# One core, mLSTM front and MLP: per-head products as scaled copies on ScalarE, and a new order of the front's events, engines and fillers

## The chip, the cores and the metric

One core of a Trainium2 chip. The metric is the device time of one execution in microseconds; of the kernel before there are three runs. The engines are named as the profile does: PE (TensorE), DVE (VectorE), ACT (ScalarE), POOL (GpSimd), SP (the queue that issues most DMAs).

## What is computed

A recurrent layer and a two-layer MLP behind it, in float32 precision (the MLP's weights come as float64):

```python
# batch 4, heads 8, seq 768, head_dim 40
m_new = np.maximum(f_gate[:, :, t] + m, i_gate[:, :, t])
f_stab = np.exp(f_gate[:, :, t] + m - m_new)
i_stab = np.exp(i_gate[:, :, t] - m_new)
C = f_stab * C + i_stab * np.einsum('bhd,bhe->bhde', vt, kt)
n = f_stab * n + i_stab * kt
h_tilde = np.einsum('bhde,bhe->bhd', C, qt)
denom = np.maximum(np.abs(nq), 1.0)        # nq = n . q
y[:, :, t] = sigmoid(o_gate) * h_tilde / denom
...
x = attn_out.transpose(0, 2, 1, 3).reshape(3072, 320)
h = x @ w_in                                # 320 x 2048
g = np.maximum(h, 0.0) + np.log1p(np.exp(-np.abs(h)))
out = g @ w_out                             # 2048 x 320
```

## The kernel before

**Steps and tiles.** The 768 positions of each batch are cut into six chunks of 128, which makes 24 steps (batch, chunk). Three steps make one tile of 384 tokens, so the MLP has eight tiles. The first six steps (tiles 0 and 1) are "plain" steps, the others "wide" ones; this change touches the plain ones most. The order of the steps is `ORDER`: (1,0), (2,0), (0,0), (3,0), then the rest by batch. Steps are numbered in that order from 0; tiles of the program are named by their batch and chunk or their step.

**One plain step.** Its inputs are `qk` (queries and keys of all heads), `vt` (values with a column of ones, and keys by token) and the decays `fb`. A scan on VectorE makes the decay matrix `pw` (L402) and the weights `gw` of the state update (L407). `gate_values` (L412) makes `vi` = values times the input gates `gT`; `state_values` (L421) makes `vw` = values times `gw`. TensorE makes scores `ga` (L435) and new state parts (L448) from `vw`; `by_decays` (L456) multiplies the scores by `pw`; `keep_states` copies the state parts to `cp`. `decay_old`, `mid_state` and `new_state` (L491 to L515) carry the state of a batch on: old state times the chunk's decay plus `cp`. `values` (L536, L544) makes `gc` from the states and from the scores. `sum_values` (L555) scales one half of `gc` by the factors `fcT` into `y1` and adds the other; `norm` makes the reciprocal `nq`; `scale_gate` (L579) multiplies the output gate by `nq`; `gated` (L584) makes `x`; TensorE transposes it to `xp`; `high_x` and `low_x` split it into a float32r high part (a cast, L719) and a low part (L676), the tile `X`.

**Products with per-head factors.** Five of these multiply each head's 40 or 41 columns by that head's factor per partition: `vi`, `vw`, `y1`, the gate, and the two decays of a state. Before, each is one `tensor_tensor` with the factors broadcast along the columns, on VectorE or POOL.

**Weights.** `single` (L238) turns a tensor of 640 float64 columns into float32 in two ScalarE steps (L248, L253) and two VectorE steps (L255, L257); `weights` and `weights_out` split it into high and low parts (casts at L719; L295, L297, L305). There are eight such pairs of tensors (w_in and w_out), 256 of the 2048 hidden columns each.

**The MLP.** `products` (L854) runs blocks of 128 hidden columns of one tile: eight matmuls into `hp` (L913), two softplus ACTIVATEs on ScalarE (high part `gh` L807, the whole in place L808), a subtraction on VectorE (`gl`, L811), and nine matmuls into three sums `po` (L877), which come two blocks later. Tile 0 runs its blocks 0 to 9 first (the weights are still arriving), then tile 1 all 16, then tile 0 the rest.

**What sets the order.** All instructions of an engine are kept in the order in which the program writes them (`in_order`, L106). The writing is driven by events in a queue: each has a time counted in TensorE's MLP matmuls (negative for the front), looked up in the table `WHEN` (L970); `tick` writes all events due. `PICK` (L1018) says which engine an event's work runs on: V VectorE, G POOL, A ScalarE, S SP. `WARM` (L1017) gives the number of filler matmuls for eleven places (`keep_warm`, L685). A change of these three tables rewrites the order on every engine.

## Time and profile before

| | us |
|---|---|
| median of 3 runs | 452.35 |
| lowest, highest run | 451.31, 455.11 |
| the profiled execution | 451.38 |
| its span in the trace | 449.6 |
| TensorE busy in the span | 436.0 |
| VectorE, ScalarE, POOL busy | 260.1, 199.5, 108.6 |

The page's busy time is what an engine worked in the span; a view by stretches gives the same for any part of it, with the granted TensorE clock (1.00 is the full clock, 2.4 GHz). A timeline lists instructions by start; instructions of one kind that follow each other are merged, and the time in brackets is idle time before the row and who ended it. A view by form gives for each kind of instruction the number, the total busy us and the mean ns of one. A matmul of float32 counts as two records.

### The profile page before, as it was taken

To read this page: it belongs to the slowest core of one execution; us is meant where nothing else is said; L and a number is where in the kernel's file an instruction comes from. 1 tells how busy PE (TensorE), PEld (TensorE's weight loads), DVE (VectorE), ACT (ScalarE), POOL (GpSimd) and SP (SyncE) were. 2 spreads that over 40 slices of the span, in tenths; PEclk is the share of its full clock that TensorE was granted. 3 is DMA by queue.
4 is the path that set the end of the run, shared out by engine and by line. 5 is a ranking of instruction groups with operands and counts; after the bars stand their busy time and mean duration, and the time that the engine had idled before them with its cause. 6 is when DMAs were issued, how large, how long until landed. Compare 5 with 4: busy or idle time off the path is not lost.

```text
span 449.6 us, 12758 instructions
## 1 busy us (share of the span) xinstructions
PE 436.0 (97%) x5348; PEld 417.4 (93%) x5348; DVE 260.1 (58%) x458; ACT 199.5 (44%) x402; POOL 108.6 (24%) x173
## 2 busy tenths in 40 slices
PE   8769999999998999999999999999999999999996
PEld 7658899999998999999999999999999999999996
DVE  6998698758784665465465465365465465332221
ACT  3576466567435333453236333463336332334332
POOL 4541465456421311211211211111211210000000
PEclk9899799999999999999999999999999999999999
DMA  6986764674435554534443533534533430001001
GB/s 201 291 257 210 241 179 139 189 190 124 122 103 159 133 160 116 170 86 122 127 127 93 139 107 89 179 79 128 127 115 102 129 104 20 23 1 44 2 1 44
DMA packets 51801, 55.93 MB, mean 124 GB/s; under 512 B 5312, under 2 KB 41824, under 8 KB 51744
## 3 DMA queue, kind: packets, MB, share of 16 engines
q1 hardware_dynamic: 48720, 51.68, 41.1%
q10 hardware_dynamic: 3024, 3.44, 2.2%
q8 instruction: 42, 0.69, 0.6%
q14 instruction: 15, 0.12, 0.1%
HBM read 46.47 MB, written 8.64 MB: 123 GB/s over the span
## 4 chain that ended last, share of the span: by engine, by line
PE 91%; DVE 3%; DMA 2%; SPq 1%; ACT 1%; issue 1%; POOL 0%; DVEq 0%; ACTq 0%; POOLq 0%
PE hp L913 40%; PE po L877 37%; PE ga L435 3%; PE gc L597 2%; PE po L688 2%; PE ga L448 2%; PE gc L609 2%; DMA yd<-y 1%; DVE pw L402 1%; DMA nw<-yd 1%; PE gc L536 0%; PE fb L386 0%; PE gc L544 0%; DVE sgi L257 0%; PE xp L666 0%
## 5 line engine op out<-in xcount | busy, mean ns | idle before, releaser
L913 PE MATMUL hp<-X,wih 128*128 128x384 f32 x768 | 181.3, 341 | 1.4 <-ACT X L719 1.4
L807 ACT ACTIVATE gh<-hp 128x384 fp32r<-128x384 f32 x128 | 62.8, 491 | 181.4 <-PE hp L913 170.7
L913 PEld LDWEIGHTS hp<-X,wih 128*128 128x128 f32 x768 | 133.0, 188 | 3.5 <-ACT X L719 1.6
L811 DVE TENSOR_TENSOR gl<-hp,gh 128x384 fp32r<-128x384 f32 x128 | 70.9, 555 | 106.3 <-ACT hp L808 106.3
L877 PE MATMUL po<-woh,gl 128*128 128x320 f32 x384 | 81.4, 312 | 1.6 <-DVE gl L811 1.6
L877 PE MATMUL po<-wol,gh 128*128 128x320 f32 x384 | 82.6, 313 | 0.0
L877 PE MATMUL po<-woh,gh 128*128 128x320 f32 x384 | 81.1, 312 | 0.0
L913 PE MATMUL hp<-X,wil 128*128 128x384 f32 x256 | 66.6, 339 | 0.0
L877 PEld LDWEIGHTS po<-woh,gh 128*128 128x128 f32 x384 | 65.5, 189 | 0.4 <-issue 0.2
L877 PEld LDWEIGHTS po<-woh,gl 128*128 128x128 f32 x384 | 62.7, 189 | 2.2 <-DVE gl L811 1.8
L877 PEld LDWEIGHTS po<-wol,gh 128*128 128x128 f32 x384 | 63.2, 189 | 0.6 <-issue 0.2
L808 ACT ACTIVATE hp<-hp 128x384 f32<-128x384 f32 x128 | 62.3, 487 | 0.0
L913 PEld LDWEIGHTS hp<-X,wil 128*128 128x128 f32 x256 | 46.3, 188 | 0.3 <-issue 0.2
L424 POOL TENSOR_TENSOR vw<-vt,gw 128x328 f32<-128x328 f32 x22 | 16.6, 753 | 111.3 <-DVE gw L407 101.3
L402 DVE TENSOR_TENSOR_SCAN pw<-fb,ident 128x512 f32<-128x512 f32 x24 | 29.5, 1227 | 0.3 <-PE fb L386 0.3
L456 DVE TENSOR_TENSOR pw<-ga,pw 128x512 f32<-128x512 f32 x23 | 15.9, 689 | 20.5 <-PE ga L448 18.1
L506 POOL TENSOR_TENSOR c<-c,cp 104x164 f32<-104x164 f32 x20 | 10.4, 518 | 71.2 <-ACT cp L719 71.1
L416 POOL TENSOR_TENSOR values_in<-vt,gT 128x328 f32<-128x328 f32 x17 | 12.9, 758 | 40.9 <-PE gc L609 19.7
L616 DVE TENSOR_TENSOR y<-gc,y 112x512 f32<-112x512 f32 x18 | 12.4, 691 | 17.2 <-PE gc L609 16.7
L435 PEld LDWEIGHTS ga<-qk 40*64 40x64 f32 x736 | 13.8, 141 | 5.0 <-issue 4.7
L642 DVE RECIPROCAL nm<-nm 128x128 f32<-128x128 f32 x18 | 17.2, 953 | 0.6
L719 ACT COPY cp<-ga 104x328 f32<-104x328 f32 (+1 forms) x21 | 8.7, 414 | 18.7 <-DVE pw L456 13.3
(150 smaller groups left out, 438.6 us busy)
## 6 DMA issues: line engine op xcount, KB each, us to landing
vt<-in_vk SPq DMA_DIRECT2D x24, 324.0 KB
qk<-in_qk SPq DMA_DIRECT2D x48, 160.0 KB
fb<-fz_d SPq DMA_DIRECT2D x42, 128.0 KB
wo<-in_w_out SPq DMA_DIRECT2D x8, 640.0 KB
wr<-in_w_in SPq DMA_DIRECT2D x8, 512.0 KB
eg<-in_oT SPq DMA_DIRECT2D x6, 576.0 KB
yd<-y SPq DMA_DIRECT2D x36, 96.0 KB
out<-ob ACTq DMA_DIRECT2D x21, 160.0 KB
```

The costliest lines, as they stand in the source:

```text
L402: nc.vector.tensor_tensor_scan(z.pw.rearrange(flat), z.fb.rearrange(flat), ident4.rearrange(flat), 0.0, ALU.mult, ALU.add)
L416: pick(f"vi{z.id}", "G").tensor_tensor(vi, z.v1, gT[:, z.c, :, z.b].unsqueeze(3).broadcast_to([128, NQ, HG, E]), op=ALU.mult)
L424: pick(f"vw{z.id}", "G").tensor_tensor(z.vw, z.v1, z.gw.unsqueeze(3).broadcast_to([128, NQ, HG, E]), op=ALU.mult)
L435: nc.tensor.matmul(z.ga[y * Q : (y + 1) * Q, x, (i * NQ + q) * Q : (i * NQ + q + 1) * Q], z.k[rows, g, ts], z.q[rows, g, ts], start=True, ...
L456: nc.vector.tensor_tensor(pw, z.ga[:, :, 0:CP0], pw, op=ALU.mult)
L616: nc.vector.tensor_tensor(y2, z.gc[0 : PP + EP, :, 0:CP0], y2, op=ALU.mult)
L642: nc.vector.reciprocal(nm, nm)
L807: nc.scalar.activation(gh, hp, AF.Softplus)
L808: nc.scalar.activation(hp, hp, AF.Softplus)
L811: nc.vector.tensor_tensor(gl, hp, gh, op=ALU.subtract)
L877: nc.tensor.matmul(po[j], a[:, j * 128 : (j + 1) * 128], w[:, f, :], start=(first and left[j] == 2), stop=(last and left[j] == 0),)
L913: nc.tensor.matmul(hp, a, r, start=(i == 0), stop=(i == len(seq) - 1))
```

## The change

**What it does.** A new helper `scaled` makes a product with per-head factors. On VectorE or POOL it is the old `tensor_tensor`; on ScalarE it is one ACTIVATE for each head (Copy, with the factor of that head as a scale read from memory): eight for `vi`, `vw`, `y1` and the gate, four for a state. All five kinds of products call it, so the decays of a state, which were fixed to POOL, and `y1`, which was fixed to VectorE, get an engine from the table too. In `products` an assertion that a block's weights are written becomes a loop that writes events until they are, and a block takes its PSUM buffer `hp` at its first matmul. The tables `WHEN`, `WARM` and `PICK` are set anew. In the new table 18 products of eight heads and 6 of four stand on ScalarE, all in plain steps or in the states that they leave. Fillers go from 45 to 38.

```diff
+    def scaled(name, default, to, of, by):
+        e = pick(name, default)
+        a, b, w = to.shape[1:]
+        if e is not nc.scalar:
+            e.tensor_tensor(to, of, by.unsqueeze(3).broadcast_to([to.shape[0], a, b, w]), op=ALU.mult)
+            return
+        for i in range(a):
+            for j in range(b):
+                e.activation(to[:, i, j], of[:, i, j], AF.Copy, scale=by[:, i, j : j + 1])
...
-        pick(f"vi{z.id}", "G").tensor_tensor(
-            vi, z.v1, gT[:, z.c, :, z.b].unsqueeze(3).broadcast_to([128, NQ, HG, E]), op=ALU.mult
-        )
+        scaled(f"vi{z.id}", "G", vi, z.v1, gT[:, z.c, :, z.b])
...
-        pick(f"vw{z.id}", "G").tensor_tensor(z.vw, z.v1, z.gw.unsqueeze(3).broadcast_to([128, NQ, HG, E]), op=ALU.mult)
+        scaled(f"vw{z.id}", "G", z.vw, z.v1, z.gw)
...
-            nc.gpsimd.tensor_tensor(heads(z.cm), heads(z.old), fl(z, 0), op=ALU.mult)
+            scaled(f"old{z.id}", "G", heads(z.cm), heads(z.old), fl(z, 0))
...
-            nc.gpsimd.tensor_tensor(heads(c), heads(z.cm) if z.c > 0 else z.cp[:, :, 0], fl(z, 1), op=ALU.mult)
+            scaled(f"new{z.id}", "G", heads(c), heads(z.cm) if z.c > 0 else z.cp[:, :, 0], fl(z, 1))
...
-        nc.vector.tensor_tensor(
-            y1[lo], gc[lo, :, 0:c0].rearrange("p x (g e) -> p x g e", e=E),
-            fc.broadcast_to([L - z.q0 * Q, 2, 4, E]), op=ALU.mult,
+        scaled(
+            f"y1{z.id}", "V", y1[lo], gc[lo, :, 0:c0].rearrange("p x (g e) -> p x g e", e=E),
+            fcT[lo, z.c, z.b].rearrange("p (x g) -> p x g", x=2),
         )
...
-        pick(f"sg{z.s}", "G").tensor_tensor(z.sig, z.sig, z.nq.broadcast_to([128, H, D]), op=ALU.mult)
+        sig = z.sig.unsqueeze(1)
+        scaled(f"sg{z.s}", "G", sig, sig, z.nq.rearrange("p h o -> p o h"))
...
+    def wait_for(names):
+        for x in names:
+            while x not in did:
+                tick(queue[0][0])
...
-                assert all(f"w{f // 2}_1_{k}" in did for k in range(5 + (w is wol)))
+                wait_for(f"w{f // 2}_1_{k}" for k in range(5 + (w is wol)))
...
-            hp = ps_h.tile([128, T], F32, tag="hp", name=f"hp{t}_{f}")
...
-                assert all(f"w{f // 2}_0_{k}" in did for k in range(5 + (i > 3 or (t, f) == (1, 0))))
+                wait_for(f"w{f // 2}_0_{k}" for k in range(5 + (i > 3 or (t, f) == (1, 0))))
+                if i == 0:
+                    hp = ps_h.tile([128, T], F32, tag="hp", name=f"hp{t}_{f}")
...
-    WARM = {0: 9, 1: 0, 2: 5, 3: 2, 4: 3, 5: 8, 6: 0, 7: 3, 8: 12, 9: 3, 10: 0}
-    PICK = {'vi0': 'V', 'vw0': 'V', 'vw2': 'V', 'sg1': 'V', 'cp2': 'V', 'sg2': 'V', 'wi00': 'G', 'mgo0': 'V', 'vi3': 'V',
...
+    WARM = {0: 10, 1: 0, 2: 2, 3: 0, 4: 2, 5: 7, 6: 8, 7: 0, 8: 6, 9: 0, 10: 3}
+    PICK = {'vi0': 'A', 'wi00': 'G', 'wm00': 'V', 'wm01': 'V', 'wl1': 'V', 'ol0': 'V', 'wl2': 'V', 'wl3': 'V', 'new4': 'V',
...
```

**What moves: ScalarE at the end of the front.** On ScalarE, the last instructions ahead of the first softplus. `X0` is the MLP input of tile 0 (its parts come from `xp1`, `xp2`, `xp0` of the first three steps), `woh` and `wih` are high parts of weights, `mag` and `sg` conversion steps, `gh0_0` the first softplus. Before:

```order
L719 CAST wih_100<-sgi1_442 128x2x256
L719 CAST wih_100<-sgi1_442 64x128 x2
L719 CAST X0_489<-xp2_0_514 128x3x128
L253 ACTIVATE sgi2_548<-wr2_356 128x640
L719 CAST X0_489<-xp0_0_553 128x3x128
L763 ACT_TABLE_LOAD
L807 ACTIVATE gh0_0_587<-hp0_0_125 128x384
L808 ACTIVATE hp0_0_125<-hp0_0_125 128x384
```

In the changed kernel (L727 is the old L719, L420 the scaled copies, L815 and L816 the old L807 and L808):

```order
L706 ACTIVATE og_123<-og_123 128x960
L727 CAST X0_551<-xp2_0_537 128x3x128
L727 CAST X0_551<-xp1_0_530 128x3x128
L771 ACT_TABLE_LOAD
L420 ACTIVATE values_in_105<-vt3_0_545,gT_93 128x41 x8
L727 CAST woh_102<-sgo0_528 128x640
L727 CAST X0_551<-xp0_0_601 128x3x128
L248 ACTIVATE magi2_625<-wr2_547 128x640
L727 COPY cp3_0_643<-ga3_0_564 104x328
L727 CAST wih_100<-sgi1_519 128x2x256
L727 CAST wih_100<-sgi1_519 64x128 x2
L253 ACTIVATE sgi2_671<-wr2_547 128x640
```

The table load for softplus and eight scaled copies of step 3's values (`values_in`) now stand ahead of the last cast of `X0`; the high parts of w_in's second tensor (`wih` from `sgi1`) and a conversion step have moved behind it.

**ScalarE among the first blocks.** On ScalarE, from the softplus of block 3 of tile 0 to that of block 4 or 5; step 4 is batch 0, chunk 1. Before:

```order
L807 ACTIVATE gh0_3_860<-hp0_3_814 128x384
L808 ACTIVATE hp0_3_814<-hp0_3_814 128x384
L719 CAST woh_102<-sgo1_625 128x640
L719 COPY cp0_1_891<-ga0_1_816 104x328
L807 ACTIVATE gh0_4_899<-hp0_4_875 128x384
L808 ACTIVATE hp0_4_875<-hp0_4_875 128x384
L719 CAST woh_102<-sgo2_787 128x640
L248 ACTIVATE magi4_928<-wr4_924 128x640
L253 ACTIVATE sgi4_931<-wr4_924 128x640
```

In the changed kernel:

```order
L815 ACTIVATE gh0_3_854<-hp0_3_843 128x384
L816 ACTIVATE hp0_3_843<-hp0_3_843 128x384
L420 ACTIVATE vw0_1_877<-vt0_1_741,gw0_1_808 128x41 x8
L420 ACTIVATE sig3_0_669<-sig3_0_669,nq3_0_839 128x40 x8
L420 ACTIVATE values_in_105<-vt0_1_741,gT_93 128x41 x8
L248 ACTIVATE mago2_911<-wo2_827 128x640
L253 ACTIVATE sgo2_913<-wo2_827 128x640
L815 ACTIVATE gh0_4_957<-hp0_4_902 128x384
L816 ACTIVATE hp0_4_902<-hp0_4_902 128x384
L248 ACTIVATE magi4_969<-wr4_832 128x640
L420 ACTIVATE c1_108<-c0_107,flast_91 104x41 x4
```

Between the softplus of block 3 and that of block 4 stand now 24 scaled copies (`vw`, the gate of step 3, `vi`) and two conversion steps, where two copies stood; four more copies (a state's decay, `c1`) come behind block 4.

**TensorE at the first block.** On TensorE, from the last transpose of the front; `hp0_0` is block 0 of tile 0, `ga3` the scores and state parts of step 3, `pg` the spread of the gates, `po3` with `ident` a filler. Before:

```order
L666 MATMUL xp0_0_553<-ident_80,x0_0_550 64x128 x2
L913 MATMUL hp0_0_125<-X0_489,wih_100 128x384 x4
L913 MATMUL hp0_0_125<-X0_489,wil_101 128x384 x2
L913 MATMUL hp0_0_125<-X0_489,wih_100 128x384 x2
L913 MATMUL hp0_1_592<-X0_489,wih_100 128x384 x4
L913 MATMUL hp0_1_592<-X0_489,wil_101 128x384
L435 MATMUL ga3_0_608<-qk3_0_494 64x64 x16
L913 MATMUL hp0_1_592<-X0_489,wil_101 128x384
```

In the changed kernel (L927 is the old L913, L456 the old L448, L696 the old L688):

```order
L456 MATMUL ga3_0_564<-vw3_0_618,vt3_0_545 40x41
L927 MATMUL hp0_0_651<-X0_551,wih_100 128x384 x4
L927 MATMUL hp0_0_651<-X0_551,wil_101 128x384 x2
L927 MATMUL hp0_0_651<-X0_551,wih_100 128x384 x2
L927 MATMUL hp0_1_679<-X0_551,wih_100 128x384 x4
L132 MATMUL pg_684<-ident_80,ig_134 64x16 x4
L137 MATMUL pg_684<-ident_80,d1_595 128x32
L132 MATMUL pg_684<-ident_80,ig_134 64x16 x4
L137 MATMUL pg_684<-ident_80,d1_595 128x32
L132 MATMUL pg_684<-ident_80,ig_134 64x16 x12
L927 MATMUL hp0_1_679<-X0_551,wil_101 128x384 x2
L696 MATMUL po3_78<-ident_80 128x128 x9
```

The scores and state parts of step 3, which stood inside blocks 1 and 2, now stand ahead of block 0; the gates' spread has moved from behind the first half of block 2 into block 1; 9 fillers follow it there, where 15 stood ahead of it and 3 behind. On SP the first tensor of w_in is now issued ahead of step 0's inputs.

## Rows read from the trace of the kernel before

**Rows 1.** The page: its first line, and TensorE's busy share.

```profile
span 449.6 us, 12758 instructions
...
PE 436.0 (97%) x5348; PEld 417.4 (93%) x5348; DVE 260.1 (58%) x458; ACT 199.5 (44%) x402; POOL 108.6 (24%) x173
```

**Rows 2.** Busy time of each engine by stretch; after the engines: clock, DMA share, GB/s.

```profile
core 0: us, PE busy (x) PEld busy (x) DVE busy (x) ACT busy (x) POOL busy (x), PEclk, DMA share, GB/s
0.00:10.00 10.00, 8.30 (x99) 7.77 (x100) 6.02 (x19) 3.21 (x6) 3.96 (x18) 1.00 0.66 192
...
20.00:30.00 10.00, 6.90 (x139) 5.50 (x132) 9.52 (x22) 5.97 (x10) 5.53 (x8) 1.00 0.84 233
...
150.00:350.00 200.00, 200.00 (x2573) 193.08 (x2572) 110.20 (x189) 82.69 (x168) 38.85 (x68) 1.00 0.45 122
```

**Rows 3.** Timeline of TensorE around the marks: start, us, engine, line, operation, tiles, count.

```profile
31.82 1.21 PE L913 MATMUL hp<-X,wih 128*128 128x384 f32 x4 [1.37 <-ACT X L719]
...
37.27 3.51 PE L688 MATMUL po<-ident 128*128 128x128 f32 x30
...
63.06 0.69 PE L435 MATMUL ga<-qk 40*64 40x64 f32 x32
...
64.12 0.44 PE L913 MATMUL hp<-X,wih 128*128 128x384 f32 x1
...
76.93 0.51 PE L913 MATMUL hp<-X,wih 128*128 128x384 f32 x2
```

**Rows 4.** The same timeline, at the one long wait behind the second mark.

```profile
145.00 0.71 PE L877 MATMUL po<-woh,gl 128*128 128x320 f32 x3 [1.56 <-DVE gl L811]
```

**Rows 5.** By half microseconds, columns as in rows 2: the lower clock's two ends.

```profile
43.50:44.00 0.50, 0.50 (x6) 0.40 (x4) 0.40 (x2) 0.00 (x0) 0.00 (x0) 0.82 0.84 291
...
50.50:51.00 0.50, 0.50 (x17) 0.43 (x10) 0.50 (x2) 0.00 (x0) 0.50 (x1) 0.85 0.87 234
```

**Rows 6.** Groups on POOL and VectorE by form: count, busy us, mean ns, idle.

```profile
L424 POOL TENSOR_TENSOR vw<-vt,gw 128x328 f32<-128x328 f32 x22 | 16.6, 753 | 111.3 <-DVE gw L407 101.3 <-PE hp L913 6.6 <-DMA vt<-in_vk 3.3
...
L580 DVE TENSOR_TENSOR og<-og,nq 128x320 f32<-128x320 f32 x2 | 1.0, 488 | 0.0
...
L402 DVE TENSOR_TENSOR_SCAN pw<-fb,ident 128x512 f32<-128x512 f32 x24 | 29.5, 1227 | 0.3 <-PE fb L386 0.3
...
L305 DVE TENSOR_TENSOR wol<-sgo,woh 128x640 fp32r<-128x640 f32 x5 | 4.7, 936 | 0.3 <-ACT woh L719 0.2
```

**Rows 7.** Timeline of ScalarE in the front: two small pairs, the last cast of X.

```profile
4.35 0.31 ACT L157 ACTIVATE fg<-fg 32x128 f32<-32x128 f32 x1 [1.08 <-DVE fg L154]
4.56 0.29 ACT L158 ACTIVATE ig<-ig 32x128 f32<-32x128 f32 x1
...
14.27 0.18 ACT L175 COPY fcT<-po 128x32 f32<-128x32 f32 x1
14.35 0.44 ACT L719 COPY cp<-ga 104x328 f32<-104x328 f32 x1
...
31.31 0.46 ACT L719 CAST X<-xp 128x384 fp32r<-128x384 f32 x1
```

**Rows 8.** Groups on ScalarE by form, columns as in rows 6.

```profile
L807 ACT ACTIVATE gh<-hp 128x384 fp32r<-128x384 f32 x128 | 62.8, 491 | 181.4 <-PE hp L913 170.7 <-issue 9.1 <-PE po L877 1.4
...
L248 ACT ACTIVATE magi<-wr 128x640 f32<-128x640 f32 x8 | 6.3, 793 | 6.6 <-DMA wr<-in_w_in 6.6
...
L719 ACT CAST wih<-sgi 128x512 fp32r<-128x512 f32 x6 | 3.7, 614 | 0.0
...
L719 ACT CAST woh<-sgo 128x640 fp32r<-128x640 f32 x6 | 4.3, 722 | 1.1 <-DVE sgo L257 1.1
...
L763 ACT ACT_TABLE_LOAD x2 | 2.6, 1283 | 0.0
...
L698 ACT ACTIVATE og<-og 128x960 f32<-128x960 f32 x2 | 2.0, 1003 | 1.2 <-DMA og<-in_o 1.1
...
L719 ACT COPY cp<-ga 104x328 f32<-104x328 f32 x18 | 7.8, 433 | 16.4 <-DVE pw L456 11.0 <-PE ga L448 5.4
```

## Prediction of the time

> **What bounds the kernel now.** I read the page's busy shares first, then the table by stretches, and last the timelines of TensorE and ScalarE around the two marks below. TensorE is busy for 436.0 us of the span of 449.6 [rows 1]. From 150 to 350 us it is busy all 200.00, with ScalarE at 82.69 [rows 2]: there, work moved between the other engines changes nothing. From 20 to 30 us it isn't: TensorE does 6.90 of 10, VectorE 9.52, ScalarE 5.97 [rows 2]. So the front is VectorE's. The marks: the first w_in product of tile 0 starts at 31.82, the first of tile 1 at 76.93 [rows 3]. What is computed behind the second mark is the same in both kernels, so the change is worth the shift of that mark, and what becomes of one wait of 1.56 us at 145 us for a `gl` of VectorE [rows 4].
>
> Between the marks lie 45.1 us. Two things there are not work for the result. One is fillers: 15 matmuls in 3.51 us at 37.27 [rows 3], 0.23 each, and 3 more. The other is the lower clock: the half-microsecond rows show a granted clock of 0.82 at 43.5 and 0.85 at 50.5 [rows 5], with thirteen rows of 0.50 between, that is 1.2 GHz for some 7.0 us, which loses 3.5.
>
> **What the change takes away and adds.** Each product with per-head factors was one instruction, 0.75 us on POOL or 0.49 on VectorE [rows 6]. Now 18 of them are 8 scaled copies on ScalarE and 6 (decays of states) are 4 copies: 168 ACTIVATEs, 128 of them ahead of the second mark.
> Ahead of its last low part of X for tile 0 VectorE loses two such products (0.49 each), a copy of `cp` that I count the same, a conversion step and two low parts of weights (0.94 each as [rows 6] has one): 4.3 us. It gains an `x` (0.5), two small subtractions (0.4 each) and the scan of step 3 with its `gw` (1.23 [rows 6] and 0.2): 2.7. That frees 1.6. But TensorE now has the state products of step 3 ahead of the first w_in product, and they wait for that scan and then for a product on POOL (0.75). So by VectorE alone the first mark stands near 31.5, hardly earlier.
> From the first mark on there are 9 fillers less (2.1); the score and state products of step 3 are done (for a later step they take from 63.06 to 64.12 [rows 3], 1.1); and if the clock stays up, 3.5 come back. 45.1 - 6.7 = 38.4, and 31.5 + 38.4 = 69.9. That is the floor which TensorE and VectorE set for the second mark, 7.0 us earlier than now.
>
> **ScalarE decides.** The trace has no copy with a factor from memory, so its price from start to start (call it p) is bounded. Below: the 32-column copy of `fcT` starts at 14.27 and the next instruction at 14.35 [rows 7], 0.08. Above: an ACTIVATE of 128 columns takes 0.31 us whole [rows 7], if nothing overlapped. Between them: that ACTIVATE starts at 4.35 and the next at 4.56 [rows 7], 0.21. I take 0.21, as the only pair of small ACTIVATEs in the trace; it has 87 columns more than a piece, and a piece has an operand more. The pair shows too that an instruction starts 0.10 before the last one ends, so every duration below counts less 0.10.
> By the columns alone a piece would be cheaper: from 640 to 384 columns ([rows 8], 0.72 and 0.49) a column is worth 0.9 ns, so 87 columns fewer make 0.13.
> Against that stands a rule of the Trainium skill, "ScalarE: Activation LUTs", What ACT_TABLE_LOAD costs: a pointer operand adds about 93 ns to an ACTIVATE, and neighbours overlap by about 93. Its price without a pointer agrees with the 0.72 us of a 640-column cast [rows 8]; the pointer's price no row here shows. By it a piece is an estimated 0.22 us from the next, and the sum below would be 1.3 us higher.
>
> Leg 1 runs from the first piece to the last cast of X for tile 0. The pieces wait for step 0's values, which SP now queues behind the first tensor of w_in: 1.5 MB in all, and the 192 GB/s of the first 10 us [rows 2] put that at 8 to 10. I take 10.0. ScalarE then has 48 pieces, and by [rows 8], less 0.10: three `cp` 1.0, a copy of factors 0.1, two Exps like the cast of 640 columns 1.3, a 64-row cast 0.2, two table loads (whole) 2.6, two sigmoids 1.8, four conversion steps 2.8, three casts of X (0.46 whole [rows 7]) 1.1, one of `woh` 0.6. That is 11.5. The cast ends at 10.0 + 11.5 + 48 p = 31.6 with p = 0.21; in the kernel before it starts at 31.31 [rows 7]. I found no input that comes later than ScalarE there.
> Leg 2 runs from there to the last cast of X for tile 1: 14 conversion steps 9.7, casts of w_in for three and a half tensors 4.0, two of `woh` 1.3, two `cp` 0.7, ten softplus pairs 7.8, gate copies 0.3, two casts of X 0.8, which is 24.6, and 80 pieces. It waits for others by an estimate from the same durations 3.6 us: 1.3 for the gate products (the first two w_in blocks stand ahead of them on TensorE), 0.9 for step 3 and block 2, 0.3 for a reciprocal, 1.1 for the last `x` and its transposes. To the first product of tile 1 another 0.2. So 28.4 + 80 p.
> Sum: 10.0 + 11.5 + 28.4 + 128 p = 49.9 + 128 p, with p = 0.21 76.8 against 76.93, 0.1 us earlier. Behind the mark 40 pieces, 8.4 us, lie under stretches where ScalarE has more than half its time free; the 1.56 us wait may go or stay, and I let it stay. The profiled execution took 451.38 us; 0.1 less is 451.3. The median of the three runs is 0.97 above the profiled one, so I forecast 452.
> Bounds of the sum: any p up to 0.156 gives the floor, 451.38 - 7.0 = 444.4. p = 0.31 gives 89.6, 12.7 later, 464.
>
> Edits at nothing. POOL and VectorE lose work in stretches where TensorE or ScalarE sets the pace; without that cover their relief is the 1.6 us above. On SP the stored gates wait for the second sigmoid, and behind them stand the second w_out tensor, the later decays and their loads. All these are first read after 38 us, so 2 or 3 us of delay are covered; a us beyond that is a us on the second mark. Blocks now take their PSUM buffer after their weights' events, which moves an allocation and no instruction. The lower clock may stay or go: nothing while ScalarE sets the pace, up to 3.5 us otherwise.
>
> **Rivals.** First, cheap pieces. At p of 0.156 or less ScalarE keeps ahead, the second mark is at 69.9 and the time 444.4, about 445 for a median. For it: the 0.08 of the small copies, the 0.13 by columns, and ScalarE's idle 4 of 10 us now. Against: none of those has a factor from memory.
> Second, slower: a piece overlaps less, or pays more for its factor. The place is the same queue, above all where the sets for `vw`, the gate and `vi` of step 4 stand in a row ahead of the softplus of block 4, while block 4's w_out products wait. From p = 0.246 the loss is over 1% (0.035 x 128 = 4.5 us); at 0.255 it is 5.6, 457, or 458 for a median. For it: the whole duration of 0.31. Against: the pairs in [rows 7] overlap.
> Third, the pieces are cheap but the new order gives its gain back: the clock falls again after the gate products (3.5) and the front is 3 us longer, since 48 pieces stand ahead of the X casts. That ends within 1% too, at 451; its mark is TensorE at 1.2 GHz after 35 us while ScalarE is idle.
>
> **How the numbers follow.** About 1% is what a measurement here can tell from no change. The forecast, with ScalarE as the pace and level with the old order, and the third rival, which ends in the same place, have 0.46 together (0.38 and 0.08). The forecast's own range is 448 to 456, p from 0.18 to 0.24. Cheap pieces have 0.36, the slower case 0.18. Faster, same and slower are these three. The 8 in 10 reach from 443, the floor less the wait at 145, to 458, the second rival at 0.255.
>
> **What would show it.** Right: pieces 0.2 us apart; the first w_in product of tile 0 between 31 and 34 us; from there to the second mark ScalarE over 90% busy, TensorE under 85%, with waits for ScalarE at the value products of steps 4 and 5; the first product of tile 1 between 75 and 79. Wrong: pieces under 0.16 apart and tile 1 before 72; pieces 0.25 or more apart; a first product of tile 0 before 29, which would say that I misread VectorE's chain; new waits of TensorE behind 150 us.

## Result and profile after

| | kernel before | changed kernel |
|---|---|---|
| median of 20 runs, us | 453.19 | 456.23 |
| lowest to highest, us | 450.87 to 457.17 | 454.27 to 458.41 |
| ratio, 95% interval | | 1.006 (1.0037 to 1.0084) |
| profiled execution, its span, us | 451.38, 449.6 | 457.89, 455.8 |

The changed kernel is 0.6% slower, 3.0 us in the medians. The time stays within 1%, as forecast, but the forecast was 0.1 us less, and it went the other way; 456.23 lies just above the forecast's own range of 448 to 456. Below, the first mark is the first w_in product of tile 0, the second mark that of tile 1. The page, and the table by stretches with the columns of [rows 2]:

```profile
span 455.8 us, 12870 instructions
...
PE 440.7 (97%) x5334; PEld 421.7 (93%) x5334; DVE 261.8 (57%) x466; ACT 230.0 (50%) x562; POOL 92.2 (20%) x149
```

```profile
20.00:30.00 10.00, 9.36 (x145) 7.54 (x142) 7.62 (x21) 9.53 (x27) 0.82 (x1) 0.50 0.91 240
50.00:60.00 10.00, 9.81 (x115) 8.63 (x114) 6.29 (x15) 9.93 (x38) 2.19 (x3) 1.00 0.84 236
60.00:70.00 10.00, 7.20 (x149) 6.46 (x148) 7.43 (x15) 10.00 (x32) 3.23 (x3) 0.83 0.57 169
150.00:350.00 200.00, 200.00 (x2574) 193.08 (x2573) 108.71 (x187) 80.11 (x166) 38.09 (x68) 1.00 0.44 122
```

From 150 to 350 us nothing has changed: TensorE is busy all the time [rows 2]. From 50 to 70 us ScalarE is now busy 19.93 of 20 and TensorE 17.01. The timeline of TensorE at the two marks, beside [rows 3]:

```profile
35.95 0.96 PE L927 MATMUL hp<-X,wih 128*128 128x384 f32 x4
40.83 3.79 PE L696 MATMUL po<-ident 128*128 128x128 f32 x18
83.82 0.84 PE L927 MATMUL hp<-X,wih 128*128 128x384 f32 x2
```

The first mark stands 4.1 us later, the second 6.9 us. Two stretches say more than the marks, up to the first one and between the two. Before:

```profile
8.00:31.82 23.82, 17.01 (x414) 14.26 (x410) 21.80 (x44) 14.51 (x25) 14.06 (x17) 0.93 0.92 271
31.82:76.93 45.11, 45.07 (x619) 40.45 (x619) 37.84 (x66) 26.47 (x53) 18.97 (x24) 0.92 0.66 199
```

Changed:

```profile
8.00:35.95 27.95, 23.19 (x489) 19.50 (x485) 22.43 (x44) 24.44 (x70) 9.80 (x11) 0.76 0.88 246
35.95:83.82 47.87, 43.06 (x539) 38.97 (x537) 34.21 (x67) 42.33 (x137) 13.29 (x15) 0.91 0.68 188
```

Between the marks TensorE had no gap; now it has 4.8 us of them, and ScalarE works 42.3 of 47.9 in place of 26.5 of 45.1. ScalarE's timeline from the softplus of block 3 to the next cast of X (a row with x8 is eight pieces, and each row starts where the last one can):

```profile
52.83 1.87 ACT L420 ACTIVATE vw<-vt,gw 128x41 f32<-128x41 f32 x8
54.60 1.85 ACT L420 ACTIVATE sig<-sig,nq 128x40 f32<-128x40 f32 x8
56.35 1.85 ACT L420 ACTIVATE values_in<-vt,gT 128x41 f32<-128x41 f32 x8
58.11 0.77 ACT L248 ACTIVATE mago<-wo 128x640 f32<-128x640 f32 x1
...
60.90 0.97 ACT L420 ACTIVATE c<-c,flast 104x41 f32<-104x41 f32 x4
61.78 0.76 ACT L253 ACTIVATE sgi<-wr 128x640 uint32<-128x640 uint32 x1
62.44 0.46 ACT L727 CAST X<-xp 128x384 fp32r<-128x384 f32 x1
```

A piece starts (58.11 - 52.83) / 24 = 0.22 us after the last. The list of TensorE's waits names what that does:

```profile
PE gc L544 <- DVE X L684: 2.8, 1, 2.8
PE xp L672 <- POOL x L592: 2.3, 2, 1.8
```

The 2.8 us are at 60.7: the values of step 4 need the PSUM buffer in which step 3's `xp` still stands (both use the one buffer of the tag `pa`). VectorE's low part frees it at 63.5 and had waited for the cast at 62.44, which stood in ScalarE's queue behind the rows above: `xp` was written by 58.5. The second wait, 1.8 us at 79.6, ends when POOL has made `x` of step 5 from a gate whose eight pieces run on ScalarE from 78.55 to 80.41.

**The same kernels profiled again.** The two profiled executions are 6.5 us apart, the medians 3.0. So both were taken once more, unchanged. For the changed kernel:

> The changed kernel once more, unchanged, on the chip of the three runs beside it. Its profiled execution lay 1.7 us above its median and that of the kernel before 1.8 below its own. If the marks are those of any execution: first product of tile 0 at 35.5 to 36.5, first of tile 1 at 83 to 84.5, ratio 1.004 to 1.009. If half of the shift of the mark was that one execution: mark at 80 to 82.5 with a time of 455 to 456.

Measured: ratio 1.0095 (1.0063 to 1.0126); the profiled execution took 455.78 us with its second mark at 82.00, as the second possibility had it. For the kernel before:

> The kernel before once more, unchanged, for a second profile of its front. If its front comes out differently from one execution to the next: first product of tile 0 at 33 to 34.5 (33.96 in the run with fewer fillers, whose order is the same up to there) in place of 31.82, mark of tile 1 at 78 to 79.5, time 452.5 to 454. If the one profile is typical: 31.5 to 32.3 and 76.5 to 77.5.

Both profiles, up to the first mark and on to the second; the kernel before:

```profile
8.00:34.38 26.38, 20.83 (x413) 17.63 (x409) 21.68 (x44) 14.66 (x25) 14.04 (x17) 0.74 0.83 248
34.38:78.03 43.65, 43.63 (x618) 39.30 (x619) 37.75 (x66) 26.46 (x53) 19.00 (x24) 0.96 0.71 204
```

the changed kernel:

```profile
8.00:35.89 27.89, 23.44 (x476) 20.03 (x474) 21.47 (x44) 24.60 (x70) 9.85 (x11) 0.69 0.85 245
35.89:82.00 46.11, 41.36 (x541) 37.28 (x537) 33.71 (x66) 42.19 (x137) 13.87 (x15) 0.94 0.70 195
```

The old front differs from one execution to the next: 31.82 at a mean clock of 0.93, 34.38 at 0.74. The profile that the prediction rests on had a fast one. In this second pair the spans are 450.8 and 453.6, and the 2.8 us are: 1.5 at the first mark, 2.5 between the marks, 1.2 less behind the second (the wait of [rows 4] is gone in both profiles of the changed kernel). That it is close to the 3.0 us of the medians is in part luck: the six executions of the changed kernel beside that profile have a median of 457.89, 5.0 above that of the kernel before, and the profiled one is among the fastest of them. So the change costs 3 to 5 us.

### The profile page after: what moved, and what is told of

It is laid out like the page before. It is cut to its first block, busy times and chain, and to the rows that moved or that the text cites. A ratio compares the mean times of both kernels' runs of the same rounds, so it can differ in the third digit from the quotient of the medians.

```text
span 455.8 us, 12870 instructions
## 1 busy us (share of the span) xinstructions
PE 440.7 (97%) x5334; PEld 421.7 (93%) x5334; DVE 261.8 (57%) x466; ACT 230.0 (50%) x562; POOL 92.2 (20%) x149
## 4 chain that ended last, share of the span: by engine, by line
PE 80%; ACT 10%; DMA 3%; issue 3%; DVE 2%; SPq 2%; POOL 0%; DVEq 0%; POOLq 0%; ACTq 0%
PE hp L927 35%; PE po L890 33%; PE ga L443 2%; PE gc L605 2%; DMA y<-fc_d 2%; PE gc L617 2%; PE ga L456 2%; PE po L696 1%; DMA vt<-in_vk 1%; ACT vw L420 1%; ACT values_in L420 1%; ACT gh L815 1%; ACT vi L420 1%; ACT sig L420 1%; ACT hp L816 1%
## 5 line engine op out<-in xcount | busy, mean ns | idle before, releaser
L927 PE MATMUL hp<-X,wih 128*128 128x384 f32 x768 | 181.8, 341 | 0.0
L815 ACT ACTIVATE gh<-hp 128x384 fp32r<-128x384 f32 x128 | 62.8, 491 | 175.6 <-PE hp L927 165.0
L927 PEld LDWEIGHTS hp<-X,wih 128*128 128x128 f32 x768 | 133.5, 189 | 1.6 <-issue 0.2
L927 PE MATMUL hp<-X,wil 128*128 128x384 f32 x256 | 66.2, 340 | 0.0
L816 ACT ACTIVATE hp<-hp 128x384 f32<-128x384 f32 x128 | 62.3, 487 | 0.0
L927 PEld LDWEIGHTS hp<-X,wil 128*128 128x128 f32 x256 | 46.7, 190 | 0.1
L416 POOL TENSOR_TENSOR vw<-vt,gw 128x328 f32<-128x328 f32 x18 | 13.8, 765 | 112.5 <-DVE gw L407 108.5
L443 PE MATMUL ga<-qk 40*64 40x64 f32 x736 | 17.0, 230 | 1.8 <-PE po L456 0.9
```

The costliest lines, as they stand in the source:

```text
L416: e.tensor_tensor(to, of, by.unsqueeze(3).broadcast_to([to.shape[0], a, b, w]), op=ALU.mult)
L443: nc.tensor.matmul(z.ga[y * Q : (y + 1) * Q, x, (i * NQ + q) * Q : (i * NQ + q + 1) * Q], z.k[rows, g, ts], z.q[rows, g, ts], start=True, ...
L815: nc.scalar.activation(gh, hp, AF.Softplus)
L816: nc.scalar.activation(hp, hp, AF.Softplus)
L927: nc.tensor.matmul(hp, a, r, start=(i == 0), stop=(i == len(seq) - 1))
```

## Experiments

A piece is one scaled copy, a set the four or eight pieces of one product. Two theories. A: ScalarE's queue sets the pace, each piece costs 0.22 us there. B: the new order, its fillers and the lower clock are slow by themselves. All marks in one table (us; the clock is the mean granted clock from 8 us to the first mark):

| run | first mark | clock | second mark | between | ratio (95%) |
|---|---|---|---|---|---|
| before, twice | 31.82, 34.38 | 0.93, 0.74 | 76.93, 78.03 | 45.1, 43.7 | 1 |
| changed, twice | 35.95, 35.89 | 0.76, 0.69 | 83.82, 82.00 | 47.9, 46.1 | 1.006, 1.0095 |
| none on ScalarE | 37.80 | 0.71 | 80.88 | 43.1 | 1.0005 (0.9987 to 1.0023) |
| constant factor | 34.26 | 0.87 | 73.06 | 38.8 | 0.9868 (0.9836 to 0.99) |
| front sets back | 37.55 | 0.71 | 85.08 | 47.5 | 1.010 (1.0067 to 1.0133) |
| later sets back | 37.02 | 0.65 | 79.92 | 42.9 | 0.9982 (0.996 to 1.0005) |
| old order, sets on ScalarE | 41.36 | 0.64 | 92.65 | 51.3 | 1.0566 (1.0492 to 1.064) |
| changed, 17 fillers less | 37.31 | 0.70 | 84.48 | 47.2 | 1.0102 (1.0051 to 1.0154) |
| changed, inputs first | 38.80 | 0.67 | 84.69 | 45.9 | 1.0118 (1.0065 to 1.0172) |
| inputs first, conversion behind | 38.06 | 0.66 | 83.88 | 45.8 | 1.0091 (1.006 to 1.0123) |
| changed, 17 fillers more | 36.72 | 0.88 | 84.05 | 47.3 | 1.0079 (1.0042 to 1.0116) |
| `fcT` first | 36.61 | 0.76 | 82.66 | 46.1 | 1.0103 (1.0032 to 1.0174) |
| 17 fillers more, later sets back | 36.97 | 0.88 | 79.69 | 42.7 | 0.9988 (0.9952 to 1.0024) |
| later sets back, 17 fillers less, inputs first | 37.31 | 0.68 | 84.17 | 46.9 | 1.0067 (1.0034 to 1.010) |
| later sets back, 17 fillers more, `fcT` first | 37.36 | 0.88 | 80.10 | 42.7 | 1.0014 (0.9982 to 1.0045) |
| later sets back, inputs first, conversion behind | 36.15 | 0.70 | 78.90 | 42.8 | 0.9991 (0.9961 to 1.0021) |
| before, 9 fillers less | 33.96 | 0.87 | 77.58 | 43.6 | 0.9987 (0.9948 to 1.0026) |
| old front, new order behind | 34.82 | 0.68 | 80.66 | 45.8 | 1.0016 (0.9972 to 1.006) |

### Which sets cost, and where

The edits take sets out of the table's "A" entries; the engine is then the one of before.

```diff
-    PICK = {'vi0': 'A', ... 'vw0': 'A', 'vi1': 'A', ... 'vi4': 'A', ...
+    PICK = {'vi0': 'V', ... 'vw0': 'V', ...
```

> The changed kernel with all 24 sets of products with factors back on the engines that the kernel before gives them (VectorE or POOL); order, fillers and all other picks as changed. Theory A, ScalarE's queue sets the pace up to the first product of tile 1 (83.82 us in the changed kernel): ScalarE loses 128 pieces of 0.22 = 28 us ahead of that mark, TensorE and VectorE decide there, the mark comes at 70 to 76 and the ratio to the kernel before is 0.975 to 0.99. Rival B, the new order, its fillers and the stretches at the lower clock are what is slow, the pieces are not: the mark stays at 80 or later and the ratio is 1.003 or more.

> The changed kernel with only the six sets of the front (48 pieces: vw of step 0, vi of steps 0 to 3, the gate of step 0) back on the engines of before. Theory A: the last cast of X for tile 0 is no longer behind 48 x 0.22 = 10.6 us of pieces; VectorE's chain sets it, near 30, the first product of tile 0 comes at 31 to 33.5 in place of 35.95, and as ScalarE still carries 80 pieces behind it the mark of tile 1 moves by the same 2 to 4 us, to 79.5 to 82; ratio to before 0.997 to 1.003. Rival B: both marks within 1 us of the changed kernel's, ratio 1.004 or more.

> The changed kernel with only the 18 later sets (80 pieces between the first product of tile 0 and the mark of tile 1, 40 behind it) back on the engines of before, the front's six sets stay on ScalarE. Theory A: the first product of tile 0 stays at 35 to 37, ScalarE loses 80 x 0.22 = 17.6 us behind it, TensorE sets the pace, and the mark of tile 1 comes 39 to 41 us after the first product of tile 0, at 74.5 to 77.5; ratio 0.983 to 0.993. Rival B: the mark stays at 80 or later, ratio 1.003 or more.

The stretch between the marks with the later 80 pieces off ScalarE, and then with only the front's 48 off:

```profile
37.02:79.92 42.90, 39.99 (x539) 36.25 (x537) 38.43 (x71) 25.38 (x53) 18.79 (x22) 0.96 0.73 210
```

```profile
37.55:85.08 47.53, 42.78 (x540) 38.82 (x537) 34.27 (x67) 42.23 (x137) 13.48 (x15) 0.91 0.69 190
```

The later sets cost 3.2 to 5.0 us between the marks (46.1 or 47.9 against 42.9, and 47.5 against 43.1 where the front's sets are off too). There Theory A has the place and the direction right. It has the size wrong: 80 pieces of 0.22 are 17.6 us of ScalarE's queue, and the stretch got 3.2 to 5.0 shorter, to 42.9 and not to 39 to 41. With the sets on VectorE and POOL TensorE waits for those. Its longest waits in the stretch, with the later sets back, and with 17 fillers more besides:

```profile
PE xp L672 <- POOL x L592: 1.4, 2, 1.2
...
PE xp L672 <- POOL x L592: 2.9, 2, 1.7
```

In the front Theory A fails: with its six sets back, the first mark comes 1.6 us later, not 2 to 4 earlier. Some 1.0 us of that is a new wait of step 3's state products for a `vw` on POOL, the same in both runs without these sets (that `vw` needs VectorE's scan, which with none on ScalarE starts at 34.87 in place of 32.75). The rest is not clear of the spread: the same front gave 35.95, 35.89 and 37.02 (the run with the later sets back), and 37.80 and 37.55 without its sets. All off together is level with the kernel before (1.0005). So Theory B falls as an account of the loss: the new order without a piece on ScalarE loses nothing. It gains nothing either, where Theory A expected 1 to 2.5%.

### The price of a piece

```diff
-                e.activation(to[:, i, j], of[:, i, j], AF.Copy, scale=by[:, i, j : j + 1])
+                e.activation(to[:, i, j], of[:, i, j], AF.Copy, scale=1.0)
```

> The changed kernel with the constant 1 in place of the factor read from memory in each scaled copy on ScalarE: the factors of those 24 sets are left out of the computation; number and order of all instructions stay. Theory A with the factor's pointer as the price: pieces start 0.13 apart in place of 0.22, 128 x 0.09 = 11.5 us less in ScalarE's queue, the mark of tile 1 moves from 83.8 to between 72 and 76, ratio to before 0.975 to 0.99. Rival C, any small ACTIVATE costs 0.22 whatever its factor: pieces stay at 0.20 to 0.22, mark and time as in the changed kernel (1.003 to 1.009). Rival B (the order is slow): pieces may be 0.13, the mark stays at 80 or later.

ScalarE, and the stretch between the marks:

```profile
49.84 1.11 ACT L420 ACTIVATE sig<-sig 128x40 f32<-128x40 f32 x8
50.85 1.12 ACT L420 ACTIVATE values_in<-vt 128x41 f32<-128x41 f32 x8
51.87 0.78 ACT L248 ACTIVATE mago<-wo 128x640 f32<-128x640 f32 x1
```

```profile
34.26:73.06 38.80, 38.01 (x539) 34.70 (x537) 34.31 (x66) 34.66 (x135) 13.47 (x15) 1.00 0.85 233
```

A piece is 0.13 now ((51.87 - 49.84) / 16), the factor in memory costs 0.09, and between the marks 38.8 are left. 80 x 0.09 = 7.2; measured are 7.3 against the second profile of the changed kernel and 9.1 against the first. That 7.2 and 7.3 agree is in part luck: the clock stays at 1.00 here, and in the changed kernel's first profile it falls to 0.50 at 64.5 and at 81.5 us, soon after the two waits named above, and at 40.5. Without its factor a piece needn't wait for one either, but such a wait is in the changed kernel's trace between the marks only once, 0.52 us for `nq`. So the price of a piece, with the order untouched, decides some 2% of the time (0.9868 against 1.006 or 1.0095). The Trainium skill, "ScalarE: Activation LUTs", What ACT_TABLE_LOAD costs, has about 93 ns for a pointer operand; the trace agrees with its 0.09.

### The same sets in the old order

```diff
-    WHEN = {...}; WARM = {...}   (changed)
+    WHEN = {...}; WARM = {...}   (before; PICK of before, the same 24 sets on 'A')
```

> The helper with the tables of the kernel before (order, fillers, picks), and only the same 24 sets put on ScalarE. Theory A (the pieces at 0.22 are the price, the new order isn't): ScalarE's queue, 66% to 89% busy around the marks in the kernel before, gets 28 us more ahead of the mark of tile 1; the mark comes at 80 to 88 in place of 76.9 and the ratio is 1.006 to 1.025. Rival D, the loss needs the new order (its later front at 36 to 38 us): in the old order the pieces fit into ScalarE's idle time, mark at 75 to 79, ratio 0.997 to 1.003.

5.7% slower: more than Theory A foresaw, and the rival that the pieces fit into idle time falls. TensorE waits three times for a `vw` on ScalarE, 7.9 us in all. The new order takes most of that cost away.

### The clock and the fillers

```diff
-    WARM = {... 6: 8, 7: 0, 8: 6, 9: 0, 10: 3}
+    WARM = {... 6: 0, 7: 0, 8: 0, 9: 0, 10: 0}
```

> The changed kernel without the 17 filler matmuls on both sides of the first product of tile 0 (8 ahead of it, 9 behind the gate products). Theory D, fillers stand on the chain there: the first product of tile 0 comes 1 to 2 us earlier (34 to 35), the second softplus and with it ScalarE's queue 3 to 5.5 us earlier, mark of tile 1 at 79 to 81, ratio 0.996 to 1.001. Rival A alone (ScalarE's queue is full all the way): mark within 1 us of 83.8, ratio 1.004 to 1.009. Rival E, the fillers hold up the clock: without them 1.2 GHz lasts longer than the 3.2 us around 42, and the mark stays or moves later.

Theory D falls and Rival E's outcome came: first mark 37.31, second 84.48, and a ratio level with the 1.0095 of the changed kernel's second measurement. At 1.2 GHz are now the stretches from 37.0 to 40.5 and from 43.75 to 47.5 us (0.51 and 0.54); from its first mark to 50 us the changed kernel has one, from 40.5 to 44.5, in its first profile and none in its second. The opposite edit puts fillers where TensorE stood idle in the front:

```diff
-    WARM = {... 1: 0, 2: 2, 3: 0, ... 9: 0}; 'k2': -279, 'k3': -234, 'k9': 13.75
+    WARM = {... 1: 4, 2: 8, 3: 4, ... 9: 3}; 'k2': -269.5, 'k3': -253.5, 'k9': -237.5
```

> The changed kernel with 17 more filler matmuls in the front, put where TensorE stood idle ahead of and inside the stretch at 1.2 GHz from 16.8 to 30.8 us (4 ahead of step 0's scores, 8 in place of 2 ahead of step 1's, 4 ahead of step 2's, 3 ahead of step 2's values). Theory F, the clock is what the late front and part of the mark are made of (half clock cost 12.0 us up to the mark in the changed kernel, 5.1 in the kernel before): that stretch shrinks to 7 us or less, first product of tile 0 at 33 to 35, mark of tile 1 at 80.5 to 83, ratio 0.998 to 1.004. Rival A (ScalarE's queue carries the front as well): stretch shorter, yet the last cast of X for tile 0 stays at 33 to 34 and the mark at 83 to 85, ratio 1.004 to 1.009.

> The same 17 more fillers, and the 18 later sets on the engines of before (six sets stay on ScalarE in the front). Theories F and A together: first product of tile 0 at 33 to 35.5, 39 to 42.9 us from there to the mark, which comes at 72 to 78; ratio 0.983 to 0.997. If neither the clock nor the sets matter: mark at 80 or later, ratio 0.998 or more.

The mean clock rises from 0.76 to 0.88, and the marks don't move earlier. The chain of waits of that run (the first of the two) shows why:

```profile
13.01 2.00 PE po L696 x16
...
17.54 1.10 PE po L696 x8
...
22.76 1.65 PE po L696 x6
```

Fillers stand in the chain themselves, 4.8 us of it (15, of which 13 are added ones), and the clock gave back an estimated 0.12 x 28.7 = 3.4, or 5.5 against the 0.69 of the second profile. With the later sets back it is the same: clock 0.65 or 0.88, mark 79.9 or 79.7. So these runs don't separate the clock from the fillers that raise it; they show that the two together gain nothing.

Between the marks the table has more to say. With all later sets on ScalarE and the fillers there unchanged, three runs have a stretch at 1.2 GHz somewhere between 40.5 and 46.5 us and take 47.3 to 47.9 (changed, front sets back, 17 fillers more); four have none and take 45.8 to 46.1 (changed again, `fcT` first, the two with inputs first). So 1.2 to 2.1 us of the loss come and go with the clock, in the same kernel too. With the later sets back that stretch is worth 0.1 to 0.4 (42.9 and 43.1 with it, 42.7 to 42.8 without), since TensorE's waits for POOL grow when it goes.

In the kernel before, as many fillers out as the change takes out:

```diff
-    WARM = {... 7: 3, 8: 12, 9: 3, 10: 0}
+    WARM = {... 7: 3, 8: 6, 9: 0, 10: 0}
```

> The kernel before (old tables, nothing on ScalarE that wasn't there) with 9 of the 18 fillers behind the first mark taken out, as many as the change takes out there. Part of theory A: with the pieces off ScalarE the new order is 2.2 us shorter between the marks than the old one, and the fewer fillers are that gain: mark at 74.5 to 75.5, ratio 0.993 to 0.997. Rival E, the fillers hold up the clock: 1.2 GHz lasts longer than the 7 us of the kernel before, mark at 76.5 to 80, ratio 0.998 to 1.008.

Between the marks 43.6, which is the 43.7 of the kernel before in its second profile. No gain that can be measured, and the prediction had 2.1 us for it.

### What holds up the front

Three moves in the table `WHEN`: step 0's inputs first on SP; the same with two conversion steps of ScalarE behind step 0's pieces; the copy `fcT` ahead of them.

```diff
-    'load0': -286, 'w0_0_0': -292, 'w0_0_1': -282, 'p7': -268
+    'load0': -296.5                                         (first)
+    'load0': -296.5, 'w0_0_0': -275.9, 'w0_0_1': -275.8     (second)
+    'p7': -280.5                                            (third)
```

> The changed kernel with only step 0's inputs issued on SP ahead of the first tensor of w_in, as before. Theory D, the late inputs hold up the front: first piece at 9.5 to 10 in place of 11.05, the first product of tile 0 1 to 1.5 us earlier, at 34.5 to 35, the mark of tile 1 at 82.3 to 83, ratio 1.002 to 1.006. Rival: the first tensor of w_in, now later, and VectorE's conversion behind it take that back, first product and mark within 0.5 us of the changed kernel's.

> The changed kernel with step 0's inputs issued first on SP as before, and now the two ScalarE steps for the first tensor of w_in behind the pieces of vw and vi of step 0, so that these don't wait behind a conversion for a later tensor. Theory H, VectorE's idle time (5.5 us in place of 2.0 between 8 us and the first product of tile 0) is what the front lost, and part of it comes from late inputs: first piece at 9.5 to 10, first product of tile 0 at 34 to 35, mark at 82 to 83, ratio 1.0 to 1.006. Rival: the order on ScalarE and the clock take it back, first product at 35.5 to 37, ratio 1.004 to 1.01.

> The changed kernel with one copy on ScalarE moved, that of the factors fcT (0.18 us), from behind the pieces of vw and vi of step 0 to ahead of them. Theory A for the front (16 pieces stand ahead of what TensorE waits for): TensorE's wait of 1.84 us for fcT ahead of step 1's scores goes, these start 1 to 2 us earlier, the stretch at 1.2 GHz gets shorter, first product of tile 0 at 33.5 to 35.5, ratio 0.998 to 1.005. Rival: step 1's scores then wait for step 0's state copy or weights instead and start within 0.5 us of 15.1; all marks and the time stay, ratio 1.004 to 1.009.

ScalarE at step 0 in the first, then in the second run:

```profile
10.53 0.77 ACT L248 ACTIVATE magi<-wr 128x640 f32<-128x640 f32 x1 [4.23 <-DMA wr<-in_w_in]
11.21 0.76 ACT L253 ACTIVATE sgi<-wr 128x640 uint32<-128x640 uint32 x1
11.87 1.85 ACT L420 ACTIVATE vw<-vt,gw 128x41 f32<-128x41 f32 x8
```

```profile
10.24 1.86 ACT L420 ACTIVATE vw<-vt,gw 128x41 f32<-128x41 f32 x8 [3.15 <-DVE gw L407]
...
15.40 0.18 ACT L175 COPY fcT<-po 128x32 f32<-128x32 f32 x1
```

In the first the pieces come 0.8 us later, since a conversion ahead of them waits for its tensor. In the second they come 0.8 us earlier, but the conversion now stands ahead of `fcT`, and TensorE's wait for that grows from 1.8 to 3.2 us. In the third that wait falls to 0.3 and others take its place (1.6 us for two `cp`, 1.0 for one more). In these three, what was moved ahead on ScalarE was paid for behind. None moved the first mark earlier.

### Versions that might beat both

Three join edits from above: the later sets back, no 17 fillers and the inputs first; the later sets back, 17 fillers more and `fcT` first; the later sets back and the inputs first with the conversion behind.

> The changed kernel with the 18 later sets on the engines of before, without the 17 fillers, and with step 0's inputs issued first. If the parts add up: first product of tile 0 at 33 to 34.5 (37.0 with the later sets moved alone, less 2 for fillers, less 1 for the inputs), from there 39 to 40 us to the mark of tile 1 (42.9 less 2 to 3.5 for the fillers), mark at 72 to 75, ratio 0.985 to 0.993. If the clock falls for longer without the fillers: mark at 76 to 79, ratio 0.994 to 1.0.

> All three together: the factors' copy first, 17 more fillers in the front, the 18 later sets back on VectorE and POOL. If the parts add up: first product of tile 0 at 32 to 34, mark of tile 1 at 71 to 76, ratio 0.98 to 0.993. If the parts share one cause, the clock, it is within 0.003 of the run with the fillers and the sets alone.

> The same order of loads, with the 18 later sets on VectorE and POOL as before. If both gains add up: first product of tile 0 at 34 to 36, 42.5 to 43 us from there to the mark, which comes at 76.5 to 79, ratio 0.988 to 0.997. If the front stays: mark at 79 to 81, ratio 0.995 to 1.001.

Marks of tile 1: 84.17, 80.10 and 78.90. In the first, without the fillers, TensorE runs at 1.2 GHz from the first mark to 49.3 us (mean clock between the marks 0.83), and the stretch takes 46.9 where the later sets back alone took 42.9. The parts don't add up in any of them. The last takes the old front and the new order behind it:

```diff
-    WHEN, PICK, WARM = changed
+    WHEN = before for events up to 21, else changed; PICK = before for steps 0 to 3, else as with the later sets back
+    WARM = {0: 9, 1: 0, 2: 5, 3: 2, 4: 3, 5: 8, 6: 0, 7: 3, 8: 6, 9: 0, 10: 0}
```

> The kernel before up to the first blocks (all events up to 21 matmuls behind the first product, with their engines; 9 fillers fewer behind the first mark), and from there the changed order with the 18 later sets on VectorE and POOL; no set on ScalarE. If the old front (32 to 34 us) and the changed order's 42.7 us between the marks and 2 us less behind them add up: mark at 74.5 to 77, ratio 0.985 to 0.996. If the changed order between the marks needs its own front: mark at 77.5 to 80, ratio 0.996 to 1.004.

1.0016 and 45.8 us between the marks, where TensorE waits 1.3 us for a `wol`, 1.2 for an `x` and 0.6 for a `pw`: behind the old front the changed order does not reach its 42.7 us, as the second possibility had it. No kernel here that does the whole work is faster than the kernel before by more than the measurement can tell; the best is the changed kernel with the later sets back, 0.9982 (0.996 to 1.0005).

## Why the prediction was wrong

**What held.** The place: ScalarE's queue between the marks is what the change costs. By the timeline the sets for `vw`, the gate and `vi` of step 4 in a row are the worst of it, with the wait of 2.8 us behind them; no run moved one of these sets alone. The test set for it was met in part: over the whole stretch ScalarE is 88% busy, not over 90, and TensorE 90%, not under 85; from 50 to 70 us it is 100 and 85. Of the cheap pieces' floor the half between the marks was right: 38.4 was worked out, 38.8 measured at 0.13 a piece. Behind the second mark nothing was lost; 0.7 and 1.2 us were gained.

**The step that failed is the sum of ScalarE's two legs**, 76.8 for the second mark; measured are 83.82 and, in the second profile, 82.00. Its largest fault is the waiting in leg 2, set at 3.6 us. What ScalarE waited for there, in the first profile:

```profile
ACT gh L815 <- PE hp L927: 2.0, 2, 1.8
ACT cp L727 <- PE ga L456: 1.4, 1, 1.4
ACT gT L223 <- PE pg L132: 1.4, 1, 1.4
ACT X L727 <- PE xp L674: 1.3, 1, 1.3
ACT sig L420 <- DVE nq L583: 0.5, 1, 0.5
```

By the sum's terms, in the same profile:
- p was taken as 0.21 from the pair of 128-column ACTIVATEs; it is 0.22. 128 x 0.01 = 1.3. The sentence on the Trainium skill had that number, and the sum by it would have been nearer.
- The first piece started at 11.05, not 10.0 (10.46 in the second profile).
- Leg 1, from there to the last cast of X, is 22.5, against 11.5 + 48 x 0.22 = 22.1: the size is right. That ScalarE alone sets it isn't shown: with none of the sets on it that cast still started at 34.68 (33.55 here), behind a `woh` that had waited 2.5 us for VectorE.
- Leg 2 had 3.6 us of waiting. ScalarE waited 6.6: 1.4 for the state parts of step 3, which stand behind 8 fillers on TensorE; 1.4 for the gates' spread; 2.0 for products, of which 1.8 come behind the 9 fillers that ran at 1.2 GHz (3.79 us); 1.3 for the last transposes; 0.5 for a reciprocal. The gates' spread was priced right (1.3), and "step 3 and block 2" at 0.9 is what failed: 3.4. I had subtracted the fillers from TensorE's bound and not asked that ScalarE waits behind those that stay. In the second profile, where the 9 fillers ran at the full clock (2.17 us), the wait for products is 0.5 and the waits are 5.0 in all.
- From the last cast to the product 1.4, not 0.2: five products of `w_out` stand between, at 1.2 GHz (granted clock 0.50 from 82 to 84 us).

These are 1.3 + 1.1 + 3.0 + 1.2 = 6.6 of the 7.0; the rest is leg 1. And the yardstick was off: the mark of 76.93 came from an execution with a fast front. With the 78.03 of the second profile the same sum would have said 1.2 us earlier.

**VectorE's chain "near 31.5"** was met in no run of the new order: 34.3 at best, with cheap pieces. The count of work held: from 8 us to its last low part of X for tile 0 VectorE works 20.8 us in place of 21.8, and 19.5 in place of 21.7 in the second pair, so 1.0 and 2.1 less where 1.6 was counted. What failed is that work was taken for time: VectorE idles 5.5 us there in place of 2.0 (6.4 in place of 4.7 in the second pair), waiting for TensorE, which waits for ScalarE or runs at the lower clock. And the first mark stands behind the state products of step 3, as the prediction said it would:

```profile
33.55 0.47 ACT L727 CAST X<-xp 128x384 fp32r<-128x384 f32 x1
...
33.37 2.05 PE L696 MATMUL po<-ident 128*128 128x128 f32 x16
35.35 0.67 PE L456 MATMUL ga<-vw,vt 64*64 64x41 f32 x32
```

The cast of X ends at 34.02 and the product starts at 35.95, behind 8 fillers and these state products, whose `vw` POOL ended at 35.04. In the kernel before, the product follows the cast at once (31.31 + 0.46, then 31.82). The 1.9 us are the same in the second profile, where the cast starts at 33.43, 0.4 earlier than in the second profile of before (33.86), and the product still comes 1.5 later. So in that pair the whole loss at the first mark stands there. What it would be without the state products ahead was not tried.

**The rivals.** The slower one was the nearest: its mechanism is what happened, at less than its price (p 0.22, not 0.246), since waits added what p did not. The third had cheap pieces, and these fell. Its other half has something to it: the new order without a piece on ScalarE is level with the old, with its first mark 3.4 us later (37.80 against 34.38 in the second profile) and no 6.7 us gained between the marks (43.1 against 45.1 and 43.7). How much of that is the clock stays open, since the one edit that raised it put fillers into the same chain.

## What to carry to other kernels

When work goes to an engine that seems idle, price it in that engine's queue, from start to start, and add up what then stands ahead of each instruction for which another engine waits; its idle share over a stretch says little. Here 48 pieces cost nothing that could be measured in the front, and 80 cost 3 to 5 us between the marks, where TensorE waits for what stands behind them. From the runs the break-even there is estimated: 42.9 with the sets elsewhere, 38.8 at 0.13, and if each us in ScalarE's queue moves the mark by one, 0.13 + 4.1 / 80 = 0.18 us a piece. And before a single profile serves as the yardstick, set its own time against the median and profile it twice: the one used here lay 1.8 us below, with a front 2.6 us earlier than in the next.

## What the runs showed of the hardware

A scaled copy that reads PSUM started sooner after the last than one that reads SBUF. The eight pieces of `y` (from `gc`) lie between the first two of these rows, those of a gate between the last two:

```profile
75.70 1.57 ACT L420 ACTIVATE y<-gc,fcT 128x41 f32<-128x41 f32 x8
77.12 0.53 ACT L815 ACTIVATE gh<-hp 128x384 fp32r<-128x384 f32 x1
...
78.55 1.86 ACT L420 ACTIVATE sig<-sig,nq 128x40 f32<-128x40 f32 x8 [0.52 <-DVE nq L583]
80.31 0.47 ACT L815 ACTIVATE gh<-hp 128x384 fp32r<-128x384 f32 x1
```

(77.12 - 75.70) / 8 = 0.18 and (80.31 - 78.55) / 8 = 0.22. The Trainium skill, "Perfetto Trace Analysis", Optimizing Scalar/DVE Operations, states some 93 ns of access for ScalarE on SBUF and 51 on PSUM; the difference of 0.04 agrees. The front's clock is not the same in each execution of one program: 0.93 and 0.74 in two of the kernel before, with 2.6 us between their first marks. The same holds behind it: in two executions of the changed kernel the same 9 fillers took 3.79 us at 1.2 GHz and 2.17 at the full clock.
